# Float32 products with v for a pair of heads in turns, split scores from the second chunk on, and own buffers for the preparation of weights

## The chip, the cores and the metric

The kernel runs on one core of a Trainium2 chip. The metric is the device time of one execution in microseconds (us), a median over runs. The engines are named as in the profile: PE (TensorE, with PEld for its weight loads), DVE (VectorE), ACT (ScalarE), POOL (GpSimd) and SP (SyncE, whose queue issues every DMA here).

## The reference, cut to what matters

```python
# q, k, v: (4, 8, 576, 64) float32;  w_in (512, 2048) and w_out (2048, 512) of both MLPs: float64
scores = q @ k.T / sqrt(64)                        # per batch and head, 576 x 576
kth    = the 32nd largest score of each row
attn   = softmax over the scores >= kth            # the others count as nothing
x      = attn @ v, heads side by side              # 2304 rows of 512
h = x @ w_in1;  x = (h - tanh(h)) @ w_out1         # first MLP
h = x @ w_in2;  y = elu(h) @ w_out2                # second MLP
```

## The kernel before

The 2304 rows are cut into six chunks of 384 tokens. Chunk ci's two MLPs run beside the attention of chunk ci+1, so there are seven stages: attention alone, five stages of both, and the last MLPs alone.

Products are made in one of two ways. As a *split* product, each float32 operand is the sum of two parts of type float32r, and TensorE makes one pass for each pair of parts. As a *plain float32* product, the operands stand as they are, and the profile shows each as two matmuls (passes) of its own. The MLPs are split everywhere: `first` makes 12 passes of 384 columns for an f-tile (128 of the 2048 hidden rows), `second` 9 passes of 512 columns. One f-tile is a step, and there are 32 steps to a chunk.

Attention goes in units of three query tiles of 128 rows: one head of a pair where a chunk lies in one batch (chunks 0, 2, 3 and 5), both heads of a pair with 192 queries each where it lies in two (chunks 1 and 4). There are eight units to a chunk, two to a pair of heads. A unit passes through:

- `load_q`, `load_k`, `split_qk`: operands of the scores. In a split unit q and k are loaded twice, onto both halves of the partitions, and ACT and POOL make the parts. `WHOLE = 2` makes chunks 0 and 1 plain float32, without parts.
- `scores`: one plain product (L253) or two split passes (L255, L256) for each half of the keys, and a copy by ACT.
- `topk_steps`: four rounds of MAX8 and MATCH_REPLACE8 on DVE, in four ticks. The last masks the weights: DVE alone (L289), or DVE, POOL and ACT in a row (L283 to L286) for the first `MASK_GP[ci]` tiles of a unit.
- `transposed`: five blocks of keys, turned by PE (L311) and copied by ACT. In a split unit ACT copies twice (L312, L315) and POOL subtracts (L317).
- `attend`: products with v, once for each unit. Plain: five blocks of two passes into 64 of the 128 PSUM partitions, one head after the other (L332). Split: `split_v` puts v's two parts side by side, and nine passes give both (L342), which ACT and DVE then add (L350, L351).
- `norm`, `finish_pair`: division by the sums of weights, once for a pair, and the two parts of x.

The weights arrive as float64. `prepare` turns a half of an f-tile into float32 in integer arithmetic and splits it: 64 times in all, in the first two stages. Its operations are ACT (L136, L137, L142), DVE (L139), POOL (L143) or DVE (L145), POOL (L146), then the split (L107, L108). Its four kinds of buffers are shared with attention's split operands (tags `kk`, `qs`, `praw`, `vv`).

A tick is a quarter of a unit's top-k search. The program issues work tick by tick, and the Tile framework's scheduler sets the order on each engine from that with its own estimate of costs; on the chip each engine then follows that order. All DMAs are on SP's queue, in order; a load that waits for its buffer holds back those behind it.

Of the kernel before, what the change touches and what calls it, by code (L numbers as in the profile page):

```python
# [11 lines left out]
U32 = mybir.dt.uint32  # L12
AF = mybir.ActivationFunctionType
# [9 lines left out]
TOPK = 32  # L23
# [5 lines left out]
N = 384  # L29
FILL = -1.0e38  # L30

# A chunk of N tokens is a list of pieces (batch, first query, number of queries).
# [17 lines left out]
LOW_GP = range(0, 24)  # L50
# [10 lines left out]
WP_BUFS = 1  # L61
KK_BUFS = 4
QS_BUFS = 2
PR_BUFS = 4
VV_BUFS = 4
S_BUFS = 6

# Blocks of keys transposed in a tick; the tick of the products with v, counted from a unit's start.
PT_PER = 3
AV_AT = 7  # L70
# Ticks from the end of a chunk's top-k searches to the start of its MLPs: of the first chunk, and of the others.
DONE0 = 4
DONE = 8
# [3 lines left out]
def tile_topk_attention_two_mlps(  # L77
# [42 lines left out]
    weights, loads = {}, [(ci, m, ft) for ci in range(len(CHUNKS)) for m in range(2) for ft in range(NF)]  # L120
# [4 lines left out]
    def prepare(m, ft, half, stay=True):  # L125
# [4 lines left out]
        raw = sb.tile([P, 576], mybir.dt.int64, tag="kk", name=f"wr{m}_{ft}_{half}", bufs=KK_BUFS)[:, :512]  # L130
        nc.sync.dma_start(raw, (w1, w2)[m][ft][:, half * 512 : half * 512 + 512])
        words = raw.bitcast(F32).rearrange("p (n w) -> p n w", w=2)
        scaled = sb.tile([P, 512], F32, tag="qs", name=f"wsc{m}_{ft}_{half}", bufs=QS_BUFS)
        sign = sb.tile([P, 768], BF16, tag="praw", name=f"wsg{m}_{ft}_{half}", bufs=PR_BUFS)[:, :512]
        w = sb.tile([P, 640], F32, tag="vv", name=f"wf{m}_{ft}_{half}", bufs=VV_BUFS)[:, :512]
        nc.scalar.activation(scaled, words[:, :, 1], copy, scale=2.0**-112)  # L136
        nc.scalar.activation(sign, words[:, :, 1], AF.Sign)  # L137
        bits, wu, low = scaled.bitcast(U32), w.bitcast(U32), words.bitcast(U32)[:, :, 0]
# [8 lines left out]
        if stay:  # L147
            wt = weight_tile(half, f"wp{m}_{ft}_{half}")
        else:
            wt = sb.tile([P, 2, 512], F32R, tag="wp", name=f"wp{m}_{ft}_{half}", bufs=WP_BUFS)  # L150
        split(wt[:, 0], wt[:, 1], w)
        nc.sync.dma_start(f(scratch[m, ft, half]), f(wt))
        return wt
# [11 lines left out]
    def hurried(u):  # L165
# [7 lines left out]
    units, x_tiles, xuns, pair_units, chunk_end = [], {}, {}, {}, []  # L173
    for ci, pieces in enumerate(CHUNKS):
        for p in range(NPAIR):
            c0 = 0
            for b, q0, nq in pieces:
                for heads in ([[0], [1]] if nq >= 256 else [[0, 1]]):
                    u = Unit()
                    u.ci, u.b, u.p, u.q0, u.heads, u.c0 = ci, b, p, q0, heads, c0  # L180
                    u.id = f"{ci}_{p}_{b}_{heads[0]}"
                    u.n = nq
                    u.whole = ci < WHOLE
                    u.last = False
                    u.rush = ci == 0 and p == NPAIR - 1
                    units.append(u)
                    pair_units.setdefault((ci, p), []).append(u)
                c0 += nq
            units[-1].last = True
        chunk_end.append(len(units))  # L190

    def load_q(u):
        u.qraw = sb.tile([P, N], F32, tag="qraw", name=f"qraw{u.id}", bufs=2)
        src = qT[u.b, 2 * u.p + u.heads[0] : 2 * u.p + u.heads[-1] + 1, :, u.q0 : u.q0 + u.n].rearrange("h d s -> d h s")
        for half in range(1 if u.whole else 2):
            nc.sync.dma_start(u.qraw[half * D : half * D + D].rearrange("d (h s) -> d h s", s=u.n), src)

    def load_k(u):
        u.kraw = {}
        for h in u.heads:  # L200
            u.kraw[h] = sb.tile([P, S], F32, tag="kraw", name=f"kraw{u.id}_{h}", bufs=2)
            for half in range(1 if u.whole else 2):
                nc.sync.dma_start(u.kraw[h][half * D : half * D + D], kT[u.b, 2 * u.p + h])

    def split_qk(u):
        """q's parts stand over each other, k's parts twice: two products give all four terms."""
# [3 lines left out]
        u.qs = sb.tile([P, 512], F32R, tag="qs", name=f"qs{u.id}", bufs=QS_BUFS)[:, :N]  # L210
        nc.scalar.activation(u.qs, u.qraw, copy)
        nc.gpsimd.tensor_sub(u.qs[D:P], u.qraw[D:P], f(u.qs[D:P]))
# [5 lines left out]
    def load_v(u):  # L218
        u.vraw = {}
        for h in u.heads:  # L220
            u.vraw[h] = sb.tile([P, NB, D], F32, tag="vraw", name=f"vraw{u.id}_{h}")
            nc.sync.dma_start(u.vraw[h], vL[u.b, :, 2 * u.p + h])

    def split_v(u):
        """The main part stands in the head's own columns of its pair, the rest in the other's."""
        if u.whole:
            return
        u.vv = {}
        for h in u.heads:
            u.vv[h] = sb.tile([P, NB, 2, D], F32R, tag="vv", name=f"vv{u.id}_{h}", bufs=VV_BUFS)  # L230
            split(u.vv[h][:, :, h, :], u.vv[h][:, :, 1 - h, :], u.vraw[h])
# [27 lines left out]
    def topk_steps(u, r):  # L259
        """Round r of the top-k search of a unit's three tiles; the last one masks the weights."""  # L260
        if r == 0:
            u.vm = sb.tile([P, 3, 2, 8], F32, tag="vm", name=f"vm{u.id}")
            u.mb = sb.tile([P, 3], F32, tag="mb", name=f"mb{u.id}")
            u.sum = sb.tile([P, 3], F32, tag="sum", name=f"sum{u.id}", bufs=6)
            u.w = [sb.tile([P, S], F32, tag="w3", name=f"w3{u.id}_{t}", bufs=3) for t in range(3)]
        if r == 1:
            u.e = [sb.tile([P, S], F32, tag="e", name=f"e{u.id}_{t}", bufs=6) for t in range(3)]

        by_pool = 0 if u.rush else MASK_GP[u.ci]

        def find(t):
            nc.vector.max(u.vm[:, t, min(r, 1)], u.s[t] if r == 0 else u.w[t])  # L272
            if r == 0 and t == 2:
                nc.gpsimd.tensor_scalar_mul(u.mb, u.vm[:, :, 0, 0], -SCALE)
            if r == 1 and t >= by_pool:
                nc.scalar.activation(u.e[t], u.s[t], AF.Exp, bias=u.mb[:, t : t + 1], scale=SCALE)  # L276

        def drop(t):
            v = u.vm[:, t, min(r, 1)]
            if r < 3:  # L280
                nc.vector.match_replace(u.w[t], v, u.s[t] if r == 0 else u.w[t], FILL)  # L281
            elif t < by_pool:
# [331 lines left out]
```

## Time and profile before

| | |
|---|---|
| median of 3 runs | 1304.95 us (1304.8 to 1308.14) |
| profiled execution: span | 1304.7 us, so 0.2 us lie around the span against the median |
| PE busy | 1222.4 us, 94% of the span |
| DVE busy | 1063.8 us, 82% |
| ACT busy | 868.7 us, 67% |
| POOL busy | 832.6 us, 64% |
| mean granted PE clock | 0.959 of full speed |

Busy shares are averages over seven stages, each with a limit of its own. A matmul's end is modelled, so the time between the starts of two matmuls tells more than the length shown for one.

### The profile page before, as it was taken

How to read it: one execution, taken by the hardware profiler on the slowest of the kernel's cores; microseconds unless marked ns; L12 is line 12 of the kernel's file. 1: busy time of each engine (PE TensorE's matmuls, PEld its weight loads, DVE VectorE, ACT ScalarE, POOL GpSimd, SP SyncE). 2: the span in 40 equal slices, each digit the busy share in tenths (PEclk: the TensorE clock that was granted, in tenths of full speed). 3: DMA queues.
4: the chain of work that ended last, by engine and by line, in shares of the span. 5: the costliest groups of instructions: out<-in, count | busy, mean ns of one | idle time of the engine just before them, and what ended most of it. 6: DMA issues, size and time to landing. Idle time of an engine off the chain costs nothing.

```text
span 1304.7 us, 20365 instructions
## 1 busy us (share of the span) xinstructions
PE 1222.4 (94%) x6384; PEld 1022.2 (78%) x6384; DVE 1063.8 (82%) x2118; ACT 868.7 (67%) x1932; POOL 832.6 (64%) x779
## 2 busy tenths in 40 slices
PE   5756899998998999999999999998999999999998
PEld 2323457775777899899998999997899989999897
DVE  7989989979999999999999899899999999110111
ACT  7767647878786766777767777668677666542333
POOL 6888309997888777667665667666666663533222
PEclk9866689998998999999999999999999999999999
DMA  6456217876587977576866677675666654577672
GB/s 217 166 180 211 83 35 236 287 250 225 173 280 250 315 238 230 171 235 211 269 213 204 219 237 257 226 238 169 220 228 232 215 193 167 203 264 259 212 253 77
DMA packets 93675, 278.83 MB, mean 214 GB/s; under 512 B 11392, under 2 KB 26240, under 8 KB 93568
## 3 DMA queue, kind: packets, MB, share of 16 engines
q1 hardware_dynamic: 93568, 277.52, 63.8%
q8 instruction: 52, 0.85, 0.3%
q14 instruction: 55, 0.45, 0.1%
HBM read 239.21 MB, written 38.27 MB: 213 GB/s over the span
## 4 chain that ended last, share of the span: by engine, by line
PE 79%; DVE 10%; ACT 6%; issue 2%; DMA 2%; POOL 1%; SPq 0%; POOLq 0%; ACTq 0%; DVEq 0%
PE h L409 30%; PE acc L443 28%; PE pt L311 5%; PE av L342 4%; PE av L332 4%; DVE vm L272 3%; PE ps L253 3%; DVE w L281 3%; DMA wr<-in_w_dram 2%; PE ps L255 2%; PE ps L256 2%; DVE wf L139 1%; DVE wf L145 1%; DVE e L289 1%; ACT y L457 1%
## 5 line engine op out<-in xcount | busy, mean ns | idle before, releaser
L272 DVE MAX8 vm<-w 128x8 f32<-128x576 f32 x432 | 320.7, 751 | 5.4
L108 POOL TENSOR_TENSOR gl<-g,gh 128x384 fp32r<-128x384 f32 x192 | 202.7, 1056 | 170.5 <-ACT gh L107 140.8
L443 PE MATMUL acc<-wt,gh 128*128 128x512 f32 x984 | 269.1, 397 | 1.1 <-ACT gh L107 1.1
L281 DVE MATCH_REPLACE8 w<-vm,w 128x576 f32<-128x576 f32 x288 | 213.1, 740 | 0.1
L443 PEld LDWEIGHTS acc<-wt,gh 128*128 128x128 f32 x984 | 177.9, 188 | 28.1 <-ACT gh L107 2.2
L257 ACT ACTIVATE s<-ps 128x288 f32<-128x288 f32 (+1 forms) x320 | 125.8, 407 | 63.8 <-PE ps L256 37.5
L317 POOL TENSOR_TENSOR pl<-pr,ph 128x384 fp32r<-128x384 f32 x128 | 134.6, 1065 | 47.8 <-ACT pr L315 46.3
L311 PE MATMUL pt<-ident,e 128*128 128x128 f32 (+1 forms) x720 | 120.3, 293 | 40.2 <-ACT e L285 32.0
L443 PE MATMUL acc<-wt,gl 128*128 128x512 f32 x492 | 148.4, 398 | 0.3 <-POOL gl L108 0.3
L409 PE MATMUL h<-xh,wt 128*128 128x384 f32 x672 | 145.6, 340 | 0.0
L107 ACT ACTIVATE gh<-g 128x384 fp32r<-128x384 f32 x192 | 101.6, 529 | 64.7 <-DVE g L422 31.6
L311 PEld LDWEIGHTS pt<-ident,e 128*128 128x128 f32 (+1 forms) x720 | 89.3, 142 | 70.6 <-ACT e L285 35.5
L312 ACT ACTIVATE ph<-pt 128x384 fp32r<-128x384 f32 (+3 forms) x240 | 115.8, 492 | 42.8 <-PE pt L311 42.0
L409 PE MATMUL h<-zh,wt 128*128 128x384 f32 (+2 forms) x720 | 141.6, 326 | 2.7 <-ACT zh L462 2.3
L272 DVE MAX8 vm<-s 128x8 f32<-128x576 f32 x144 | 107.9, 749 | 29.2 <-ACT s L257 28.9
L422 DVE SCALAR_TENSOR_TENSOR g<-t,h 128x384 f32<-128x384 f32 x96 | 52.3, 545 | 94.3 <-ACT t L415 90.9
L409 PEld LDWEIGHTS h<-xh,wt 128*128 128x128 f32 x672 | 118.8, 188 | 7.9 <-issue 0.8
L409 PEld LDWEIGHTS h<-zh,wt 128*128 128x128 f32 x720 | 118.0, 189 | 8.3 <-ACT zh L462 3.5
L289 DVE SCALAR_TENSOR_TENSOR e<-s,vm,e 128x576 f32<-128x576 f32 x118 | 115.0, 979 | 2.8 <-ACT e L276 2.4
L253 PE MATMUL ps<-kraw,qraw 64*128 64x288 f32 x224 | 97.7, 561 | 19.0 <-ACT ph L312 9.5
L281 DVE MATCH_REPLACE8 w<-vm,s 128x576 f32<-128x576 f32 x144 | 106.6, 741 | 0.0
L427 DVE TENSOR_TENSOR g<-h,t 128x384 f32<-128x384 f32 x84 | 46.0, 548 | 69.8 <-ACT t L412 68.8
(90 smaller groups left out, 2558.5 us busy)
## 6 DMA issues: line engine op xcount, KB each, us to landing
wt<-w SPq DMA_DIRECT2D x328, 512.0 KB, 4.2
wr<-in_w_dram SPq DMA_DIRECT2D x64, 512.0 KB, 5.0
w<-wp SPq DMA_DIRECT2D x64, 512.0 KB, 4.1
kraw<-in_kT_dram SPq DMA_DIRECT2D x104, 144.0 KB, 3.9
vraw<-in_vL_dram SPq DMA_DIRECT2D x64, 160.0 KB, 3.7
qraw<-in_qT_dram SPq DMA_DIRECT2D x80, 96.0 KB, 3.8
out_dram<-o SPq DMA_DIRECT2D x5, 768.0 KB, 5.0
out_dram<-o SPq DMA_DIRECT2D x3, 256.0 KB, 2.2
```

Source lines behind the costliest of these rows:

```text
L107: nc.scalar.activation(hi, src, copy)
L108: nc.gpsimd.tensor_sub(lo, src, f(hi))
L253: nc.tensor.matmul(pt[:, :HS], u.qraw[0:D, qc], u.kraw[h][0:D, cs], start=True, stop=True)
L257: nc.scalar.activation(s[lo:hi, cs], pt[lo:hi, :HS], copy)
L272: nc.vector.max(u.vm[:, t, min(r, 1)], u.s[t] if r == 0 else u.w[t])
L281: nc.vector.match_replace(u.w[t], v, u.s[t] if r == 0 else u.w[t], FILL)
L289: nc.vector.scalar_tensor_tensor(u.e[t], u.s[t], v[:, 7:8], u.e[t], op0=ALU.is_ge, op1=ALU.mult, accum_out=u.sum[:, t : t + 1])
L311: nc.tensor.transpose(pt[:kn, t * P : t * P + P], u.e[t][:, k0 : k0 + kn], ident)
L312: nc.scalar.activation(u.ph[:kn, blk], pt[:kn, :N], copy)
L317: nc.gpsimd.tensor_sub(low, raw[:kn], f(u.ph[:kn, blk]))
L409: nc.tensor.matmul(h[:, cs], wv[:, wi, kt], xs[:, kt, cs], start=(a == 0), stop=(a == len(jobs) - 1))
L443: nc.tensor.matmul(acc[ci, m][:, t], gx[:, t * P : t * P + P], wt[:, wi], start=(ft == 0 and k == 0), stop=(ft == NF - 1 and k == 2),)
```

## The change

1. `WHOLE` goes from 2 to 1: chunk 1's scores are split like those of chunks 2 to 5.
2. Products with v are plain float32 in all chunks. `split_v`, the second copy, POOL's subtraction and the sum of two parts are gone.
3. `attend` runs once for a pair, behind the pair's last unit, with the two heads' passes in turns, block by block; they go to the two halves of the PSUM partitions. One copy takes both. `ph` gets two buffers, v four.
4. `MASK_GP` is gone: DVE masks every tile (L289 of before).
5. `prepare` gets buffers of its own (three, two and two), writes the scaled words in place, lets ACT round all low words, and joins the words in one DVE instruction. Early tiles use the weights' own buffers.
6. `norm` adds 1e-9 on POOL and takes one reciprocal for a pair. `GATE_GP` is [0, 0, 1, 1, 1, 2]. The result of a chunk is stored tile by tile.
7. Loads of v are issued three ticks after a unit's start (before: one tick in split units, four in plain ones; in the first chunk's last unit one, as before), and loads of q and k eight ticks ahead in chunk 1 (before: six).

```diff
-WHOLE = 2
-MASK_GP = [3, 0, 0, 1, 0, 0]
-GATE_GP = [0, 1, 0, 0, 0, 2]
+GATE_GP = [0, 0, 1, 1, 1, 2]
...
+RAW_BUFS = 3
+KK_BUFS = 3
+VR_BUFS = 4
+PH_BUFS = 2
+WHOLE = 1
...
-        nc.vector.tensor_scalar(wu, bits, 3, None, op0=ALU.logical_shift_left)
-        if m * NF + ft in LOW_GP:
-            i32 = mybir.dt.int32
-            nc.scalar.activation(low.bitcast(i32), low, copy, scale=2.0**-29 * (1 - 2.0**-20), bias=-0.5 + 7.5 * 2.0**-20)
-            nc.gpsimd.tensor_tensor(w.bitcast(i32), w.bitcast(i32), low.bitcast(i32), op=ALU.add)
-        else:
-            nc.vector.scalar_tensor_tensor(wu, low, 29, wu, op0=ALU.logical_shift_right, op1=ALU.bitwise_or)
+        nc.scalar.activation(low.bitcast(I32), low, copy, scale=2.0**-29 * (1 - 2.0**-20), bias=-0.5 + 7.5 * 2.0**-20)
+        nc.vector.scalar_tensor_tensor(
+            w.bitcast(U32), scaled.bitcast(U32), 3, low, op0=ALU.logical_shift_left, op1=ALU.bitwise_or
+        )
         nc.gpsimd.tensor_mul(w, w, sign)
...
+        for c0, heads in pieces.items():
+            n = heads[0][0].n
+            pt = bank("at", f"av{ci}_{p}_{c0}", 3)
+            for blk, (_, kn) in enumerate(KBLK):
+                for h in range(2):
+                    v, cs = heads[h]
                     nc.tensor.matmul(
-                        pt[main, : u.n], u.vraw[h][:kn, blk], u.ph[:kn, blk, cs], start=(blk == 0), stop=(blk == NB - 1)
+                        pt[h * D : h * D + D, :n],
+                        v.vraw[h][:kn, blk],
+                        v.g.ph[:kn, blk, cs],
+                        start=(blk == 0),
+                        stop=(blk == NB - 1),
                     )
...
+            if hurried(u):
+                nc.vector.tensor_mul(xun[:, xs], pt[:, :n], u.rs[:, xs])
+            else:
+                nc.scalar.activation(xun[:, xs], pt[:, :n], copy)
...
+                nc.gpsimd.tensor_scalar_add(r[:, at : at + len(v.g.tiles)], v.g.sum[:, : len(v.g.tiles)], 1e-9)
...
+        nc.vector.reciprocal(r[:, :at], r[:, :at])
...
+            on(before, t0 + (1 if hurried(u) else 3), lambda u=u: load_v(u))
...
+            if u.last:
+                on(ends, t0 + 7, lambda u=u: norm(u.ci, u.p, u))
+                on(ends, t0 + 7, lambda u=u: attend(u))
+                on(ends, t0 + 7, lambda u=u: finish_pair(u))
```

## Rows read from the trace of the kernel before

**Rows 1.** Busy time by stage: window, length, engines (x instructions), PE clock, DMA.

```profile
0.00:186.80 186.80, 129.46 (x335) 64.55 (x336) 168.47 (x343) 121.30 (x263) 117.73 (x105) 0.76 0.45 153
...
186.80:445.40 258.60, 247.65 (x1244) 188.80 (x1244) 245.22 (x460) 201.09 (x425) 216.98 (x180) 0.97 0.73 244
445.40:1164.40 719.00, 711.91 (x4125) 649.84 (x4125) 634.90 (x1290) 498.94 (x1150) 459.96 (x458) 1.00 0.67 220
```

**Rows 2.** The chain that ended last: start us, us, what; products with v.

```profile
181.91 2.72 PE av L332 x8
...
185.31 0.79 PE av L332 x2
...
554.91 1.59 PE av L342 x9
...
828.56 2.19 PE av L342 x18
```

**Rows 3.** PE in order of time, chunk 1: 20 plain passes, two heads.

```profile
247.25 3.84 PE L332 MATMUL av<-ph,vraw 128*64 128x192 f32 x20
```

**Rows 4.** PE in order of time, chunk 4: L373's passes in 64-column halves.

```profile
827.62 0.94 PE L373 MATMUL rt<-ident,r 128*64 128x128 f32 x16
```

**Rows 5.** PE matmuls by form that overlap 827.60 to 827.70 us.

```profile
L373 PE MATMUL rt<-ident,r 128*64 128x128 f32 x1 | 0.3, 322 | 0.0
L373 PE MATMUL rt<-ident,r 128*64 128x64 f32 x1 | 0.3, 269 | 0.0
```

**Rows 6.** PE in order of time, chunk 2: two split passes of the scores, next matmul.

```profile
645.21 0.29 PE L255 MATMUL ps<-kk,qs 128*128 128x288 f32 x1
...
645.48 0.39 PE L443 MATMUL acc<-wt,gh 128*128 128x512 f32 x1
```

**Rows 7.** DVE groups, 186.8 to 445.4 us: busy us, mean ns, idle before.

```profile
L139 DVE TENSOR_SCALAR wf<-wsc 128x512 uint32<-128x512 uint32 x41 | 35.6, 869 | 0.8 <-ACT wsc L136 0.8
L289 DVE SCALAR_TENSOR_TENSOR e<-s,vm,e 128x576 f32<-128x576 f32 x28 | 31.2, 1121 | 1.7 <-ACT e L276 1.7
...
L145 DVE SCALAR_TENSOR_TENSOR wf<-wr,wf 128x512 uint32<-128x512 uint32 x16 | 17.8, 1111 | 0.0
...
L359 DVE TENSOR_SCALAR r<-sum 128x3 f32<-128x3 f32 x10 | 4.6, 459 | 0.5 <-PE rt L373 0.5
```

**Rows 8.** Durations of two DVE lines: min/median/max ns, over the whole span.

```profile
L289 DVE SCALAR_TENSOR_TENSOR e<-s,vm,e x118: 781/810/1841, 143.9 to 1109.6; 128x576 f32<-128x576 f32 x118
...
L145 DVE SCALAR_TENSOR_TENSOR wf<-wr,wf x16: 667/1106/1830, 337.7 to 414.9; 128x512 uint32<-128x512 uint32 x16
```

**Rows 9.** POOL groups, 186.8 to 445.4 us.

```profile
L108 POOL TENSOR_TENSOR wp<-wf,wp 128x512 fp32r<-128x512 f32 x45 | 63.2, 1405 | 18.5 <-ACT wp L107 18.4
L146 POOL TENSOR_TENSOR wf<-wf,wsg 128x512 f32<-128x512 f32 x41 | 51.9, 1270 | 4.8 <-DVE wf L145 4.0 <-ACT wsc L136 0.7
...
L143 POOL TENSOR_TENSOR wf<-wf,wr 128x512 int32<-128x512 int32 x25 | 34.7, 1390 | 2.8 <-DVE wf L139 2.8
L108 POOL TENSOR_TENSOR kk<-kraw,kk 128x576 fp32r<-128x576 f32 x6 | 8.8, 1460 | 0.0
```

**Rows 10.** ACT groups, 186.8 to 445.4 us.

```profile
L142 ACT ACTIVATE wr<-wr 128x512 int32<-128x512 uint32 x21 | 14.0, 667 | 0.0
...
L107 ACT ACTIVATE kk<-kraw 128x576 fp32r<-128x576 f32 x7 | 4.8, 688 | 1.1 <-DVE wf L145 1.0
```

**Rows 11.** DVE groups, 0 to 186.8 us.

```profile
L139 DVE TENSOR_SCALAR wf<-wsc 128x512 uint32<-128x512 uint32 x23 | 15.5, 673 | 0.5 <-ACT wsc L136 0.5
L283 DVE TENSOR_SCALAR w<-s,vm 128x576 f32<-128x576 f32 x18 | 13.5, 751 | 0.0
...
L359 DVE TENSOR_SCALAR r<-sum 128x3 f32<-128x3 f32 x8 | 3.5, 443 | 0.0
L281 DVE MATCH_VALUE_LOAD w<-vm,s 128x8 f32 x27 | 2.1, 79 | 5.0 <-ACT e L285 4.9
```

**Rows 12.** Waits of SP's queue: us in total, times, longest us.

```profile
SPq L222 <- PE av L332: 55.5, 22, 9.8
```

More of the change, by code (lines that the diff above doesn't have):

```diff
@@ L40 @@
 ]
-WHOLE = 2
-MASK_GP = [3, 0, 0, 1, 0, 0]
-GATE_GP = [0, 1, 0, 0, 0, 2]
-LOW_GP = range(0, 24)
+SIZES = [sum(n for _, _, n in c) for c in CHUNKS]
+NMAX = max(SIZES)
+GATE_GP = [0, 0, 1, 1, 1, 2]
 EARLY = range(12, 16)
@@ L119, in tile_topk_attention_two_mlps, with prepare @@
     }
-    weights, loads = {}, [(ci, m, ft) for ci in range(len(CHUNKS)) for m in range(2) for ft in range(NF)]
+    weights, loads = {}, [(ci, m, ft) for ci in range(len(SIZES)) for m in range(2) for ft in range(NF)]
     def weight_tile(half, name):
         return sb.tile([P, 2, 512], F32R, tag=f"w{half}", name=name, bufs=(WI_BUFS, WO_BUFS)[half])
-    def prepare(m, ft, half, stay=True):
-        raw = sb.tile([P, 576], mybir.dt.int64, tag="kk", name=f"wr{m}_{ft}_{half}", bufs=KK_BUFS)[:, :512]
+    def prepare(m, ft, half):
+        raw = sb.tile([P, 512], I64, tag="wr", name=f"wr{m}_{ft}_{half}", bufs=RAW_BUFS)
@@ L163, in load_next @@
                 nc.sync.dma_start(f(wt), f(scratch[m, ft, half]))
+    class Unit:
+        pass
+    class Group:
+        pass
+    units, groups, pair_units, pair_end, chunk_end = [], [], {}, {}, []
+    x_tiles, xuns = {}, {}
+    for ci, size in enumerate(SIZES):
+        for p in range(NPAIR):
+            row = []
+            c0 = 0
+            for b, q0, n in CHUNKS[ci]:
+                for heads in ([[0], [1]] if n >= 256 else [[0, 1]]):
+                    u = Unit()
+                    u.ci, u.b, u.p, u.q0, u.heads, u.c0, u.n = ci, b, p, q0, heads, c0, n
+                    u.id = f"{ci}_{p}_{b}_{q0}_{heads[0]}"
+                    u.whole = ci < WHOLE
+                    u.last = False
+                    u.k = n * len(heads) // P
+                    row.append(u)
+                c0 += n
+            pair_units[ci, p] = row
+            units += row
+            cuts, k = [], 0
+            for u in sorted(row, key=lambda u: -u.k):
+                for g in cuts:
+                    if sum(v.k for v in g) + u.k <= 3:
+                        g.append(u)
+                        break
+                else:
+                    cuts.append([u])
+            for us in cuts:
+                g = Group()
+                g.units, g.at, g.id = us, len(groups), f"{ci}_{p}_{us[0].id}"
+                g.tiles = [(u, t) for u in us for t in range(u.k)]
+                g.rush = ci == 0 and p == NPAIR - 1
+                for u in us:
+                    u.g, u.j0, u.rush = g, sum(v.k for v in us[: us.index(u)]), g.rush
+                groups.append(g)
+            for u in groups[-1].units[-1:]:
+                u.last = True
+                pair_end[ci, p] = u
+        chunk_end.append(len(groups))
@@ L165, in hurried @@
     def hurried(u):
         return u.rush and u.last
-    class Unit:
-        pass
[L173 to L190, printed above, removed]
@@ L220, in load_v @@
         for h in u.heads:
-            u.vraw[h] = sb.tile([P, NB, D], F32, tag="vraw", name=f"vraw{u.id}_{h}")
+            u.vraw[h] = sb.tile([P, NB, D], F32, tag="vraw", name=f"vraw{u.id}_{h}", bufs=VR_BUFS)
             nc.sync.dma_start(u.vraw[h], vL[u.b, :, 2 * u.p + h])
[L224 to L231, printed above, removed]
     def segments(u, t):
@@ L257, in scores, with topk_steps @@
                 nc.scalar.activation(s[lo:hi, cs], pt[lo:hi, :HS], copy)
-    def topk_steps(u, r):
+    def topk_steps(g, r):
+        k = len(g.tiles)
         if r == 0:
[L262 to L265, printed above, removed]
+            g.vm = sb.tile([P, 4, 2, 8], F32, tag="vm", name=f"vm{g.id}")
+            g.mb = sb.tile([P, 4], F32, tag="mb", name=f"mb{g.id}")
+            g.sum = sb.tile([P, 4], F32, tag="sum", name=f"sum{g.id}", bufs=8)
+            g.w = [sb.tile([P, S], F32, tag="w3", name=f"w3{g.id}_{j}", bufs=W_BUFS) for j in range(k)]
@@ L266, in topk_steps @@
         if r == 1:
[L267 to L276, printed above, removed]
@@ L370, in norm @@
                 continue
-            for t in range(3):
+            for t in range(v.k):
                 for lo, hi, h, c in segments(v, t):
@@ L433, in second @@
     def second(ci, m, ft):
+        nt = SIZES[ci] // P
         if ft == 0:
@@ L437, in second @@
         gh, gl = parts.pop((ci, m, ft))
-        jobs = [(k, t) for k in range(3) for t in range(3)]
+        jobs = [(k, t) for k in range(3) for t in range(nt)]
         if ft == NF - 1:
@@ L466, in store @@
         a = acc.pop((ci, 1))
-        y = sb.tile([P, 3, 512], F32, tag="y", name=f"o{ci}", bufs=1)
-        rows = out[ci * N : ci * N + N].rearrange("(t p) e -> p t e", p=P)
-        last = ci == len(CHUNKS) - 1
-        for t in range(3):
-            nc.scalar.activation(y[:, t], a[:, t], copy)
-            if last:
-                nc.sync.dma_start(rows[:, t], y[:, t])
-        if not last:
-            nc.sync.dma_start(rows, y)
+        nt = SIZES[ci] // P
+        y = [sb.tile([P, 512], F32, tag="y", name=f"o{ci}_{t}", bufs=Y_BUFS) for t in range(SIZES[ci] // P)]
+        spans, c0 = [], 0
+        for b, q0, n in CHUNKS[ci]:
+            while n:
+                k = min(n, P - c0 % P)
+                spans.append((c0 // P, c0 % P, k, b * S + q0))
+                c0, q0, n = c0 + k, q0 + k, n - k
+        for t in range(nt):
+            nc.scalar.activation(y[t], a[:, t], copy)
+            for at, r0, k, row in spans:
+                if at == t:
+                    nc.sync.dma_start(out[row : row + k], y[t][r0 : r0 + k])
     def step_parts(i):
@@ L557, in tile_topk_attention_two_mlps @@
             if j == 0:
-                for t in range(3):
-                    on(tick, -4, t, lambda u, t=t: scores(u, t))
+                for do in mid.get(tick, ()):
+                    do()
             b()
```

282 lines of the change are left out of this document (136 added, 146 removed).

## The prediction

> **What bounds the kernel now.** I began with busy time by stage, cut where the first chunk's x is ready (186.8 us) and where the results of chunks 0 and 4 leave (445.4 and 1164.4 us) [rows 1]. The reader is to see three different kernels in it. From 445.4 to 1164.4 us, the four stages that hold the MLPs of chunks 1 to 4 and the attention of chunks 2 to 5, PE is busy for 711.9 of 719.0 us and DVE for 634.9: PE alone sets the time, a microsecond more of PE work is a microsecond of time, and work taken from the other engines returns at most the 7.1 us in which PE stood. From 186.8 to 445.4 us (MLP of chunk 0, attention of chunk 1, most of the weights' preparation) PE has 247.7, DVE 245.2, POOL 217.0 and ACT 201.1 of 258.6 us. There PE and DVE bound together, so relief of one is worth only what the other allows. Before 186.8 us DVE leads with 168.5 and PE, half idle, is granted 0.76 of its clock. The last stage, MLPs alone, isn't touched. Second, I read the prices of the products with v in the chain and in PE's order of time [rows 2, 3], and whether passes on the two halves of the PSUM partitions overlap anywhere [rows 4, 5]. Third came DVE, POOL and ACT by line in the second and the first stage [rows 7 to 11].
>
> **The products with v: what a pass costs.** At the end of the first stage a plain head of 384 queries takes 2.72 us for its eight passes over full blocks and 0.79 us for the two over the last, half block: 3.5 us, 0.34 us for a full pass [rows 2]. A split head takes 1.59 us for nine passes [rows 2]. So one plain head costs 2.2 times a split one, and everything hangs on whether two heads in turns run at once. Nothing in the kernel before makes these products in turns. The nearest row is L373, which also sends plain passes alternately wide into the two halves: 16 passes, eight of 128 columns and eight of 64, in at most 0.94 us [rows 4]. One after another, at 0.34 us for 384 columns, they would take 8 x 0.113 + 8 x 0.057 = 1.36 us. And in the first 0.1 us there starts, beside the first pass of 128 columns, one of 64 [rows 5], though the program has two of 128 first: it can only be of a later product. So the halves overlap in this kernel. In chunk 1 the program lists one head's ten passes and then the other's; 20 passes of 192 columns take 3.84 us [rows 3], no better than 20 x 0.17 = 3.4 us in a row. Turns are what is new. I take full overlap plus 0.2 us for filling and draining: 3.7 us a pair of 384, about 2.0 us a piece of 192 (half of 3.84, and a little). Bounds: 3.5 us, and 7.0 us for no overlap.
>
> The Trainium skill (PSUM — Partial Sum Buffer, "Engine vs sequencer instructions") says that matmuls start and complete in program order. The pass of 64 columns that starts within the first 0.1 us speaks against it here; by that rule turns would still overlap, with one pass of lag in every group.
>
> **What that adds and takes, by stage.** Chunks 2, 3 and 5 have 12 pairs: before 2 x 1.59 = 3.2 us, after 3.7, so +6 us; without overlap +3.8 x 12 = +46. Chunk 4: 18 passes of two heads take 2.19 us before [rows 2], eight times 17.5 us; after 8 x 2.0 = 16, so -1.5; without overlap 8 x 3.84 = 30.7, so +13. Chunk 1: eight times 3.84 = 30.7 before, 16 after, so -15; without overlap 0. Chunk 0 isn't PE-bound; only its last pair counts, where before just the second head's 3.5 us stood at the end and now the pair's 3.7 does: nothing with overlap, +3.5 without.
>
> **Chunk 1's scores.** 64 plain products of two passes of 288 columns, 0.34 x 288/384 = 0.255 us each, are 33 us. Split, two passes take 0.27 us from the first start to the next matmul [rows 6], 64 x 0.27 = 17: PE -16 us. With -15 from above PE has some 217 of the second stage's work left, and DVE alone bounds it.
>
> **The second stage on DVE.** The preparation there now takes 41 L139 (35.6 us) and 16 L145 (17.8) [rows 7]; after, one instruction of L145's kind each. L145 lasts from 0.667 us to 1.83, mean 1.11 [rows 7, 8]; which it is goes with POOL's business, as for L289, whose median is 0.81 over all and whose mean here is 1.12. POOL stays as busy: it loses 25 L143 (34.7 us) and gains chunk 1's parts of k and q, 16 x 1.46 and 8 of two thirds of that, 31 us [rows 9]. I take 1.05 us: 43 us for 53.4, -10 (bounds -26 and -8). L359 leaves, -4.6 [rows 7]. DVE goes from 245 to 230 us; at today's share of 95% the stage would take 243 us, -15. But ACT, 201 us now, gains 20 roundings of 0.667 us and the copies of k (16 x 0.688) and q (8 of some 0.46) [rows 10]: 28 us, so 229 of 243, 94% where it had 78%. Every matmul's result goes through ACT, so some of the gain is lost in its queue: I take -12. Bounds: 0, and -28 if DVE's 13 us of idling goes too.
>
> **The first stage on DVE.** 23 L139 (15.5 us) become 23 instructions of 0.8 us (between L145's 0.667 and 1.11, POOL having lost its additions): +3. 18 L283 (13.5 us) become L289 at its median with the sum read out, 0.9 us: +2.7. Gone are L359 (3.5) and the 4.9 us in which DVE waited for the masked weights' exponentials [rows 11]. Together -3; bounds -8 and +5.
>
> **At nothing.** In the four PE-bound stages POOL's subtractions, ACT's second copies and DVE's sums leave engines that PE covers; I credit 2 of the 7.1 us in which PE stood. Loads of v move two ticks later, and in chunk 4 the next pair's may reach SP's queue ahead of the products that free its buffer. Such waits exist, 55.5 us in 22, 9.8 at most [rows 12]; behind them stand weight loads, five f-tiles ahead, some 27 us, so nothing shows; without that cover each would cost its length, at most 9.8. Doubled q and k loads of chunk 1 use DMA that is busy 0.73 of the time [rows 1]. Fewer buffers for the preparation cost nothing while a half f-tile, every 258.6/41 = 6.3 us, holds a buffer over POOL's 1.27 and 1.41 us [rows 9] and the steps between; two buffers cover some 12 us.
>
> **Sum.** 1304.7 - 3 - 12 + 6 - 1.5 - 2 = 1292.2 us, and 0.2 around the span: 1292.
>
> **Rivals.** *No overlap.* The second head's passes wait for the first's, by a shared path that L373's short passes don't fill. Stages three to six get +59, the first +0.5, the second gains 10 on the scores and DVE: about 1352 us. Rows 4 and 5 speak against it; it decides as soon as a pair takes more than 4.7 us, where the 12 pairs alone eat the gain. *ACT holds the second stage.* Its 28 us more leave that stage where it is: 1304.7 - 3 + 4.5 - 2 = 1304 us. For it speaks that four engines are near full; against it, that ACT has 57 us free there now. *Passes start in program order.* A lag of 0.34 us on 12 pairs and 0.17 on chunk 4's eight pieces adds 5 us: 1298. This is what the Trainium skill's rule above would make of it.
>
> **Chances.** Forecast 0.60 (own range 1282 to 1301, the bounds of the first two stages drawn in); no overlap 0.10; ACT 0.20 (1299 to 1312); program order 0.05; more than the forecast, DVE's idling gone too, 0.05 (1276 to 1282). A range of 1276 to 1312 leaves out the first rival and the tails, somewhat under 2 in 10. Faster or slower by over 0.3%, about what a measurement of this kernel can tell from no change, is below 1301 or above 1309. Faster: 0.55 of the forecast, 0.04 of program order, 0.05, and 0.02 of ACT's, 0.66. Slower: 0.10, 0.07 of ACT's, and 0.03 for an order of work that the scheduler makes worse, 0.20. The same: 0.14.
>
> **What would show it.** Right: in chunks 2 to 5 the 20 passes of a pair span 3.5 to 4 us; chunk 1's scores show two short passes; the result of chunk 0 leaves near 430 us; the four stages behind take 719 to 724 us. Wrong: a pair near 7 us; a second stage of 255 us or more with ACT, or POOL behind it, ending PE's and DVE's waits; SP's waits for v in front of stalled weight loads; a first stage longer than 190 us, with DVE waiting for a buffer of the preparation.

## The result, and the profile after

The kernel after takes 1316.49 us (median of four runs, 1312.89 to 1318.28) against 1306.09 us for the kernel before beside it: a ratio of 1.0075, 95% interval 1.0056 to 1.0093. It is slower; 1292 us was forecast, and the range ended at 1312. The profiled execution's span is 1314.6 us.

Busy time by stage, of the kernel after, as in [rows 1]: the low part of the first chunk's x is written at 187.1 us (before at 189.2, 2.4 us behind the cut in [rows 1]), the results of chunks 0 and 4 leave at 436.8 and 1174.4 us.

```profile
0.00:187.10 187.10, 115.20 (x345) 60.49 (x346) 175.44 (x354) 120.28 (x245) 74.37 (x78) 0.78 0.49 158
187.10:436.80 249.70, 219.45 (x1257) 186.21 (x1256) 240.52 (x448) 217.13 (x456) 204.98 (x175) 0.93 0.77 258
436.80:1174.40 737.60, 727.15 (x4148) 620.80 (x4147) 587.13 (x1181) 420.94 (x929) 271.85 (x294) 1.00 0.67 215
1174.40:1314.60 140.20, 132.82 (x680) 117.99 (x678) 15.20 (x27) 46.85 (x95) 37.54 (x37) 0.99 0.63 208
```

Between these events the first stage went from 189.2 to 187.1 us, -2.1, and the second from 256.2 to 249.7, -6.5; the four PE-bound stages went from 719.0 to 737.6, +18.6, and the last one stayed. So 8.6 us were won up to chunk 0's result, and over twice that was lost behind it, where DVE (634.9 to 587.1 us), ACT and POOL all had less to do and PE more (711.9 to 727.2).

Those stages hold the 12 pairs of chunks 2, 3 and 5 and the four of chunk 4. PE in order of time, the kernel after, two of the 12 pairs (start us, us, line, operation; L337 are the products with v, L417 and L453 the MLPs' passes, L409 and L443 before):

```profile
445.84 2.15 PE L337 MATMUL av<-ph,vraw 128*64 128x384 f32 x10
447.92 1.66 PE L453 MATMUL acc<-wt,gh 128*128 128x512 f32 x6
449.42 0.86 PE L453 MATMUL acc<-wt,gl 128*128 128x512 f32 x3
450.21 0.87 PE L337 MATMUL av<-ph,vraw 128*64 128x384 f32 x4
451.01 1.66 PE L453 MATMUL acc<-wt,gh 128*128 128x512 f32 x6
452.51 0.86 PE L453 MATMUL acc<-wt,gl 128*128 128x512 f32 x3
453.30 1.65 PE L337 MATMUL av<-ph,vraw 128*64 128x384 f32 x6
454.88 0.62 PE L417 MATMUL h<-xh,wt 128*128 128x384 f32 x2
...
495.58 3.59 PE L337 MATMUL av<-ph,vraw 128*64 128x384 f32 x20
499.11 0.97 PE L417 MATMUL h<-xh,wt 128*128 128x384 f32 x4
```

The second pair runs as forecast: 3.52 us from its first start to the next matmul, for 20 passes. The first is cut in three by 18 passes of the second MLP. The same view between 495.57 and 495.70 us, by form, is the counterpart of [rows 5]: two passes of the pair start there at once.

```profile
L337 PE MATMUL av<-ph,vraw 128*64 128x384 f32 x2 | 0.5, 537 | 0.0
```

Their starts lie 7 ns apart, and the next two follow after 0.37 us. So a pair is ten rounds of two passes. They are one pass of each head: in the first experiment below, where the heads don't take turns, no two passes start so close.

For every pair I took the time from its first start to the matmul behind it, less 0.231 us for each pass of 512 columns (0.174 for one of 384) that stands in between:

| products with v, chunks 2 to 5 | before | after | forecast of the difference |
|---|---|---|---|
| 24 heads, or 12 pairs, of chunks 2, 3, 5 | 38.4 us (1.57 to 1.70 a head) | 51.6 us: four uncut pairs at 3.52, eight cut ones at 4.50 to 4.89 | +6 |
| chunk 4 | 16.2 us | 15.4 us (3.85 for 40 passes) | -1.5 |
| sum | 54.6 us | 67.0 us | +4.5 |

Whole pairs would make 42.2 us of the 51.6, so the cuts cost 9.4 us, 1.0 to 1.4 for each cut pair. The shortest cut shows where it goes; PE in order of time, the kernel after:

```profile
679.75 0.86 PE L337 MATMUL av<-ph,vraw 128*64 128x384 f32 x2
680.54 0.96 PE L453 MATMUL acc<-wt,gl 128*128 128x512 f32 x3
681.43 3.59 PE L337 MATMUL av<-ph,vraw 128*64 128x384 f32 x18
684.95 0.79 PE L417 MATMUL h<-xh,wt 128*128 128x384 f32 x3
```

The two passes in front are both passes of one head's first product: they start one after the other, 0.37 us apart, while the other head's product stands behind the cut. The trace of line L337, 679.5 to 680.4 us (ns at the least, median, most; first and last start):

```profile
L337 PE MATMUL av<-ph,vraw x2: 486/512/537, 679.8 to 680.1; 128*64 128x384 f32 x2
```

Among the 18 passes behind the cut two more start alone, 0.32 us apart, near the end, so those 18 take ten rounds and not nine. The pair has twelve rounds for ten. In each of the eight cut pairs just four passes start alone, whether it is cut once or twice: two rounds more, some 0.65 us. The rest is the change between passes on half the columns and on all 128: three passes of the MLP, 0.69 us at their usual pace, take 0.89 here, and the first round after the change is longer. A pair cut once takes 0.98 to 1.00 us more than a whole one, a pair cut twice 1.34 to 1.37. So of the 9.4 us some 5 are passes left without a partner and some 4 the twelve cuts themselves.

### The profile page after: what moved, and what is told of

Read it like the earlier page. It is cut to its first block, busy times and chain, and to the rows that moved or that the text cites. A ratio compares the mean times of both kernels' runs of the same rounds, so it can differ in the third digit from the quotient of the medians.

```text
span 1314.6 us, 19819 instructions
## 1 busy us (share of the span) xinstructions
PE 1194.6 (91%) x6424; PEld 985.5 (75%) x6424; DVE 1018.3 (77%) x2008; ACT 805.2 (61%) x1722; POOL 588.7 (45%) x584
## 4 chain that ended last, share of the span: by engine, by line
PE 66%; DVE 14%; ACT 8%; DMA 6%; issue 3%; POOL 3%; SPq 0%; POOLq 0%; ACTq 0%; DVEq 0%
PE h L417 27%; PE acc L453 25%; DVE vm L286 5%; PE av L337 5%; DVE w L296 5%; DMA wr<-in_w_dram 4%; PE pt L319 4%; PE ps L268 2%; PE ps L269 2%; DVE e L298 2%; DVE wf L143 1%; ACT wr L142 1%; ACT s L270 1%; POOL wp L112 1%; ACT wr L141 1%
## 5 line engine op out<-in xcount | busy, mean ns | idle before, releaser
L453 PE MATMUL acc<-wt,gh 128*128 128x512 f32 x984 | 266.7, 398 | 1.8 <-ACT gh L111 1.8
L453 PEld LDWEIGHTS acc<-wt,gh 128*128 128x128 f32 x984 | 180.0, 188 | 35.3 <-ACT gh L111 2.5
L319 PE MATMUL pt<-ident,e 128*128 128x128 f32 (+1 forms) x720 | 123.5, 296 | 74.9 <-DVE e L298 53.3
L111 ACT ACTIVATE gh<-g 128x384 fp32r<-128x384 f32 x192 | 100.5, 525 | 82.6 <-DVE g L431 42.2
L453 PE MATMUL acc<-wt,gl 128*128 128x512 f32 x492 | 150.3, 400 | 0.3 <-POOL gl L112 0.3
L320 ACT ACTIVATE ph<-pt 128x384 f32<-128x384 f32 (+1 forms) x240 | 109.3, 488 | 64.9 <-PE pt L319 63.8
L417 PE MATMUL h<-zh,wt 128*128 128x384 f32 (+2 forms) x720 | 142.6, 328 | 3.5 <-ACT zh L472 3.0
L417 PE MATMUL h<-xh,wt 128*128 128x384 f32 x672 | 141.1, 339 | 0.7 <-DVE g L431 0.7
L298 DVE SCALAR_TENSOR_TENSOR e<-s,vm,e 128x576 f32<-128x576 f32 x144 | 136.8, 957 | 3.0 <-ACT e L290 0.9
L417 PEld LDWEIGHTS h<-zh,wt 128*128 128x128 f32 x720 | 118.6, 190 | 14.3 <-ACT zh L472 3.9
L417 PEld LDWEIGHTS h<-xh,wt 128*128 128x128 f32 x672 | 117.4, 188 | 9.8 <-issue 2.4
L290 ACT ACTIVATE e<-s,mb 128x576 f32<-128x576 f32 x144 | 101.6, 770 | 28.7 <-POOL mb L288 28.4
L337 PE MATMUL av<-ph,vraw 128*64 128x384 f32 (+3 forms) x640 | 107.5, 440 | 0.0
L453 PEld LDWEIGHTS acc<-wt,gl 128*128 128x128 f32 x492 | 90.1, 188 | 20.8 <-POOL gl L112 1.9
```

Source lines behind the costliest of these rows:

```text
L111: nc.scalar.activation(hi, src, copy)
L290: nc.scalar.activation(u.e[t], u.s[t], AF.Exp, bias=g.mb[:, j : j + 1], scale=SCALE)
L298: nc.vector.scalar_tensor_tensor(u.e[t], u.s[t], v[:, 7:8], u.e[t], op0=ALU.is_ge, op1=ALU.mult, accum_out=g.sum[:, j : j + 1])
L319: nc.tensor.transpose(pt[:kn, j * P : j * P + P], v.e[t][:, k0 : k0 + kn], ident)
L320: nc.scalar.activation(g.ph[:kn, blk, :nq], pt[:kn, :nq], copy)
L337: nc.tensor.matmul(pt[h * D : h * D + D, :n], v.vraw[h][:kn, blk], v.g.ph[:kn, blk, cs], start=(blk == 0), stop=(blk == NB - 1),)
```

## The experiments

Two theories stood at the start. By *cut*, the halves overlap and PE's loss comes from foreign passes within a pair. By *turns*, the halves hinder each other and the price of the pair itself is wrong. For the second stage DVE, ACT, POOL and the buffers of the preparation were candidates.

**One head after the other.** The kernel after, with the two loops over blocks and heads exchanged:

```diff
-            for blk, (_, kn) in enumerate(KBLK):
-                for h in range(2):
+            for h in range(2):
+                for blk, (_, kn) in enumerate(KBLK):
```

> The changed kernel with one head's ten passes listed before the other's. If turns are what lets two heads run at once, a pair of 384 queries takes 7.0 us for 3.5, chunk 4's eight pieces 31 us for 15.5: the four PE-bound stages get some 45 to 57 us longer, the kernel takes 1360 to 1375 us. If passes on the two halves overlapped in any order, nothing changes (1316).

Measured: 1377.86 us, ratio 1.0552 (1.0534 to 1.0570). PE in order of time, an uncut pair of this kernel:

```profile
609.12 7.09 PE L337 MATMUL av<-ph,vraw 128*64 128x384 f32 x20
616.14 1.14 PE L417 MATMUL h<-zh,wt 128*128 128x384 f32 x5
```

7.02 us in a row, 3.52 in turns: the overlap is complete, and it is worth 61 us of the kernel. Nine pairs of 384 are cut here too, and cost only 0.24 to 0.42 us more than uncut ones, against 1.0 to 1.4 in turns: with no partners to lose, this is the price of the change alone. One that is cut as the pair at 679.75 us was takes 7.36 us without the three MLP passes, for 7.02:

```profile
504.77 0.86 PE L337 MATMUL av<-ph,vraw 128*64 128x384 f32 x2
505.56 0.96 PE L453 MATMUL acc<-wt,gl 128*128 128x512 f32 x3
506.45 6.45 PE L337 MATMUL av<-ph,vraw 128*64 128x384 f32 x18
512.83 0.80 PE L417 MATMUL h<-xh,wt 128*128 128x384 f32 x3
```

**Products ahead of the MLP's last part.** In the program a tick issues the third part of its MLP step, `c()`, just ahead of the pair's products. Here the products go first:

```diff
-            c()
             if j == 0:
                 for do in ends.get(tick, ()):
                     do()
+            c()
```

> The changed kernel with a pair's products issued ahead of the second MLP product of the same tick, where the changed one issues them behind it; the scheduler then leaves the passes together. Theory of the cut groups: the passes with v are parted by MLP passes, each cut drains the array and leaves a head's passes alone; then the products of chunks 2, 3 and 5 fall from 18.5 to some 14.5 us a chunk and the kernel takes 1304 to 1308 us. Theory of the price: plain passes cost that by themselves, and nothing changes (1316).

Measured: 1308.5 us, ratio 1.0008 (0.9999 to 1.0018): 8 us of the loss are gone. PE in order of time, the pair that was cut at 679.75 us in the kernel after, and the windows of this kernel's second stage and of the four PE-bound ones:

```profile
676.50 3.59 PE L337 MATMUL av<-ph,vraw 128*64 128x384 f32 x20
680.02 0.96 PE L453 MATMUL acc<-wt,gl 128*128 128x512 f32 x3
```

```profile
185.20:439.70 254.50, 220.00 (x1280) 184.91 (x1278) 244.31 (x458) 221.54 (x466) 207.38 (x180) 0.95 0.77 257
439.70:1165.70 726.00, 715.89 (x4125) 622.78 (x4125) 585.66 (x1171) 414.91 (x918) 267.79 (x290) 0.99 0.68 217
```

Eleven of the 12 pairs are whole now, at 3.52 us. The last is cut by 42 MLP passes into 8 and 12; there no pass starts alone, and it takes 3.91 us. The products with v of the 16 pairs take 58.0 us for 67.0, and the four stages 726.0 for 737.6. So the theory of the cut stands. The second stage is 4.8 us longer, and holds the first of the 12 pairs now, 3.5 us that left the four. Of the 7.0 us by which the four still exceed the kernel before, 3 are time in which PE stands (10.1 us for 7.1); PE's longest waits come at the turn from the first MLP to the second. The rest isn't told apart. PE's waits from the end of chunk 0 to that of chunk 4 (us in total, times, longest), of the kernel before, of the kernel after, and of this one:

```profile
PE yt L460 <- ACT y L457: 1.8, 3, 0.7
```

```profile
PE yt L470 <- ACT y L467: 3.9, 4, 2.4
PE h L417 <- ACT zh L472: 2.7, 3, 1.2
PE ps L268 <- DVE zl L473: 2.5, 2, 2.0
```

```profile
PE yt L470 <- ACT y L467: 5.9, 4, 2.7
PE h L417 <- ACT zh L472: 2.4, 2, 1.2
```

**Split products where one head fills a unit.** The kernel after, with the kernel before's transposes, split of v and split products in chunks 2, 3 and 5, and the pairs in turns in chunks 0, 1 and 4:

```diff
+PARTS = (2, 3, 5)
...
-                on(ends, t0 + 7, lambda u=u: attend(u))
+                on(ends, t0 + 7, lambda u=u: (attend_parts if u.ci in PARTS else attend)(u))
```

> The changed kernel with the split products with v of the kernel before in chunks 2, 3 and 5 alone; chunks 0, 1 and 4 keep the plain ones in turns. If the loss lies in those products (cut or price), the four PE-bound stages go back to some 720 us and the kernel takes 1298 to 1303 us, faster than before. If it lies elsewhere (attention's pace, loads, order of the MLPs), it stays at 1312 to 1318.

Measured: 1295.04 us, ratio 0.9921 (0.9905 to 0.9937). It beats both kernels. Windows, second stage and the four behind it:

```profile
183.80:437.50 253.70, 220.47 (x1261) 186.50 (x1260) 242.63 (x452) 220.78 (x466) 211.45 (x187) 0.94 0.78 259
437.50:1151.90 714.40, 707.15 (x4120) 640.73 (x4119) 608.87 (x1203) 475.34 (x1077) 406.19 (x427) 1.00 0.69 220
```

714.4 us for 719.0 before and 737.6 after, with 134 us more work on POOL than after: POOL has the room. The split heads are cut here as well, by up to 24 passes, and take 1.55 to 1.67 us apart from these, cut or not. A cut costs them nothing that can be read: they use all 128 columns, as the MLPs do, and have no partner to lose.

**Split products, ahead of `c()`.** The two edits above together; and, on top, a fourth buffer for the raw weights:

> The third experiment's kernel (split products with v in chunks 2, 3 and 5, plain ones in turns elsewhere) with the products issued ahead of the second MLP product, as in the second experiment. If cuts cost split products little, since they need no turns, and only chunks 1 and 4 gain: 1292 to 1297 us, as the third. If the order itself saves time everywhere: 1286 to 1291.

> The seventh's kernel with four buffers for the raw words, room for which comes from letting the small part of the products share a tag. If late raw words hold the second stage, 3 to 8 us below the seventh; else the same.

Measured: 1304.62 us (0.9981 to 0.9999) and 1311.61 us (1.0030 to 1.0054). With hardly a cut left that costs anything, the new order only does harm: the second stage takes 260.1 us for 253.7. The fourth buffer came with another edit (the products' second part shares a buffer with the transposes), so the 7 us that the two cost aren't told apart.

**Chunk 1's scores.** The kernel after with `WHOLE = 2`, plain scores in chunk 1 as before:

> The changed kernel with chunk 1's scores plain again (WHOLE = 2): PE gets 16 us more in the second stage, ACT some 15 and POOL some 31 us less. If DVE alone bounds that stage, as the prediction had it, nothing is lost: 1312 to 1317, the less POOL in DVE's way the better. If the split scores carried the second stage's gain, it gives it back: 1322 to 1330.

Measured: 1320.9 us, ratio 1.0112 (1.0098 to 1.0126), 4.4 us above the kernel after, between the two ranges expected. The second stage takes 253.2 us for 249.7 and the third 185.2 for 180.4; split scores in chunk 1 are a gain, a small one for 16 us of PE's work.

**Buffers of the preparation.** `RAW_BUFS` 3 to 5, the buffers of `wsg` and `wf` 2 to 4:

> The changed kernel with more buffers for the preparation of weights: five for the raw words (three) and four each for the signs and the words (two). If the second stage is held by raw words that land late because their buffer is freed late, it gets 4 to 10 us shorter: 1306 to 1312 us. If DVE's own work holds it, nothing changes: 1314 to 1318.

Measured: 1328.99 us, ratio 1.0173 (1.0158 to 1.0188). Both expectations missed: more buffers are worse. First stage 193.6 us (187.1), second 250.5 (249.7), third 184.6 (180.4). In the first stage, which DVE leads, two more joins run (23 for 21) and joins and masks take longer, 22.0 and 29.1 us for 18.3 and 27.4: 5.4 of its 6.5 us. Why they do wasn't tested.

**DVE's join, taken apart again.** One instruction of DVE's becomes a shift on DVE and an addition on POOL, for all 64 halves:

```diff
-        nc.vector.scalar_tensor_tensor(
-            w.bitcast(U32), scaled.bitcast(U32), 3, low, op0=ALU.logical_shift_left, op1=ALU.bitwise_or
-        )
+        nc.vector.tensor_scalar(w.bitcast(U32), scaled.bitcast(U32), 3, None, op0=ALU.logical_shift_left)
+        nc.gpsimd.tensor_tensor(w.bitcast(I32), w.bitcast(I32), low.bitcast(I32), op=ALU.add)
```

> The changed kernel with the words joined by a shift on DVE and an addition on POOL, as the kernel before did for 48 of the 64 halves, here for all 64. The prediction's term for the preparation: the join on DVE costs or saves little against a shift that waits for POOL, but POOL gets some 65 to 80 us more in the first two stages, three quarters of it in the second, where it has 49 us free: 1318 to 1328 us. If POOL has room enough, 1312 to 1317.

Measured: 1345.21 us, ratio 1.0301 (1.0288 to 1.0315). Window of the second stage:

```profile
179.40:487.80 308.40, 248.68 (x1382) 203.03 (x1381) 299.88 (x591) 244.76 (x520) 275.60 (x239) 0.93 0.65 219
```

DVE is busy for 97% of a stage that is 59 us longer, POOL for 89%. Little of DVE's work was for chunks 0 and 1: chunk 1's attention ended at 358 us (399 after, 423 before), and DVE searched for chunk 2, with 167 MAX8 in the stage for 122, until chunk 0's MLP was done. A busy share near full is no sign that the stage waits for DVE.

**Chunk 1's MLP three ticks sooner.** `DONE = [4, 5, 8, 8, 8, 8]` for `[4, 8, 8, 8, 8, 8]`, first in the kernel after, then with the split products:

> The changed kernel with the second chunk's MLPs due three ticks earlier (DONE 5 for 8), so that chunk 0's MLP steps are packed into 33 ticks for 36 and less of chunk 2's top-k search comes among them. Theory of running ahead: the 15 us that DVE gained in the second stage went in part into top-k search of chunk 2, which is worth nothing since PE alone holds the later stages; then the result of chunk 0 leaves 5 to 12 us earlier and the kernel takes 1304 to 1312 us. If the preparation holds chunk 0's MLP steps, 1313 to 1318.

> The third experiment's kernel (split products with v in chunks 2, 3 and 5) with the same three ticks: by running ahead 1283 to 1290 us, by the preparation 1293 to 1297.

Measured: 1318.58 us (1.0082 to 1.0109) and 1299.02 us (0.9926 to 0.9955): nothing gained. The second stage took 252.2 us and holds 87 + 30 MAX8 for 91 + 31 after (on replaced tiles, and on scores). So the new `DONE` kept only five of them out, and says little on whether it costs that DVE runs ahead with chunk 2.

**Heads in a row in chunks 0 and 1 alone**, with the split products elsewhere:

> The third experiment's kernel with the heads one after the other in chunks 0 and 1, so that turns are left in chunk 4 alone: PE gets 13 to 15 us more in the second stage and 3.5 at the end of the first. If DVE holds the second stage, as the prediction had it, 1296 to 1300 us; if PE's relief made its gain, 1306 to 1312.

Measured: 1313.53 us, ratio 1.0061 (1.0047 to 1.0075), 18 us above the split products with turns. The second stage takes 265.7 us for 253.7, the first 189.7 for 183.8, and PE is busy in the second for 236.9 us instead of 220.5. PE's relief was worth most of its length there, though PE stands for 30 of 250 us in the kernel after.

**Taking work from one engine at a time.** Three kernels that leave something out, each from the kernel after: ACT's rounding, POOL's product with the sign, and one of the three MATCH_REPLACE8 of a tile on DVE.

```diff
-        nc.scalar.activation(low.bitcast(I32), low, copy, scale=2.0**-29 * (1 - 2.0**-20), bias=-0.5 + 7.5 * 2.0**-20)
         nc.vector.scalar_tensor_tensor(
-            w.bitcast(U32), scaled.bitcast(U32), 3, low, op0=ALU.logical_shift_left, op1=ALU.bitwise_or
+            w.bitcast(U32), scaled.bitcast(U32), 3, scaled.bitcast(U32), op0=ALU.logical_shift_left, op1=ALU.bitwise_and
         )
```

(DVE's join stays, and reads the scaled words in place of the rounded ones.)

> The changed kernel without ACT's rounding of the low words (the weights miss their last three bits): ACT gets some 41 x 0.57 = 23 us less in the second stage. If ACT's queue holds that stage (187.1 to 436.8 us now), it gets 10 to 20 us shorter; if DVE or POOL does, under 5.

```diff
-        nc.gpsimd.tensor_mul(w, w, sign)
```

> The changed kernel without POOL's product with the signs (the weights lose their signs): POOL gets some 43 x 1.29 = 55 us less in the second stage, and stands less in DVE's way. If POOL holds the stage, it gets 15 us or more shorter; if ACT does, under 5; if DVE does, some 5 to 10, by the shorter joins.

```diff
+            if r == 2:
+                return
```

> The changed kernel without the third of the top-k search's three replacements (24 largest are kept for 32): DVE gets some 24 to 30 x 0.66 = 16 to 20 us less in each of the first five stages of attention. If DVE holds the second stage, as the prediction had it, that gets 14 to 20 us shorter and the first some 10 to 15; if ACT or POOL does, under 5. The later stages don't change, since PE alone holds them.

Measured: 1309.6 us (1.0010 to 1.0034), 1308.36 us (1.0003 to 1.0030) and 1295.67 us (0.9889 to 0.9963). Windows of the second stage, one fence for each, with the third stage behind in the first and the first stage ahead in the last; the kernel after has 987 PE instructions in its third stage, which takes 180.4 us:

```profile
186.00:435.50 249.50, 224.76 (x1304) 188.99 (x1303) 249.35 (x478) 203.28 (x434) 214.74 (x181) 0.95 0.75 254
435.50:609.60 174.10, 171.65 (x940) 146.30 (x939) 141.49 (x287) 95.12 (x211) 59.04 (x66) 1.00 0.68 233
```

```profile
183.20:423.00 239.80, 210.58 (x1214) 177.09 (x1213) 225.37 (x426) 208.81 (x441) 145.64 (x129) 0.94 0.78 266
```

```profile
0.00:170.50 170.50, 114.10 (x345) 62.12 (x346) 155.86 (x300) 118.65 (x245) 74.34 (x78) 0.77 0.53 174
170.50:422.40 251.90, 223.46 (x1280) 186.84 (x1279) 231.64 (x405) 221.25 (x467) 206.34 (x181) 0.94 0.75 257
```

With less on ACT the stage stays (249.5 us), but 47 of PE's instructions for chunk 2 moved into it, and the third stage, where PE bounds, is 6.3 us shorter. With less on POOL the second loses 10 us, of which the third gives 6 back (186.7 for 180.4), with 43 instructions moved the other way. With less on DVE the first stage loses 16.6 us, the second gains 2, and the third loses 2. So the second stage can't be judged by its length alone. Second and third together take 430.1 us after, 423.6 with less on ACT, 426.5 with less on POOL, 430.4 with less on DVE. DVE bounds the first stage, as argued, and its searches don't bound the second; ACT isn't ruled out there. Behind the third stage the last kernel still gains some: all four PE-bound stages take 730.2 us for 737.6, where nothing was expected.

**Moving POOL's work to DVE.** Two kernels from the split products: the low parts of chunk 1's k on DVE, and the low part of every second prepared half on DVE.

> The third experiment's kernel with the low parts of chunk 1's k made by DVE: POOL gets some 16 x 1.46 = 23 us less, most of it in the second stage, DVE some 16 x 0.7 = 11 us more. If POOL's queue holds that stage and DVE's fullness is work that runs ahead: 1286 to 1292 us; if DVE holds it: 1299 to 1308.

> The third experiment's kernel with the low part of every second prepared half made by DVE (those not prepared early): POOL gets some 28 x 1.4 = 39 us less in the first two stages, DVE some 28 x 0.65 = 18 us more. By POOL's queue 1285 to 1292 us, by DVE 1300 to 1312.

Measured: 1305.24 us (0.9979 to 1.0003) and 1323.62 us (1.0122 to 1.0155). The second stage takes 268.3 and 279.1 us for 253.7, second and third together 438.6 and 446.0 for 429.1. Had POOL alone held it, both had to gain.

## Why the prediction was wrong

**A pair's 20 passes stay together: the step that failed first.** "I take full overlap plus 0.2 us ... 3.7 us a pair" was right for the overlap (3.52 us, and 7.02 without) and for chunk 4 (3.85 for a pair's 40 passes, 4.0 forecast; the kernel before takes 2.0 us there for 18 passes, not the 2.19 of the one row read, so 0.8 us were won and not 1.5). It took for granted that a pair's passes would stand side by side in PE's order. They are issued in the same tick as an MLP step, and the scheduler put 3 to 42 foreign passes into eight of the 12 pairs. It does so before as well, which I could have seen, but there a cut is free. PE in order of time, the kernel before: a split head's nine passes with nine of the MLP among them, its first and the matmul behind it.

```profile
575.78 0.34 PE L342 MATMUL av<-ph,vv 128*128 128x384 f32 x1
...
579.43 0.33 PE L409 MATMUL h<-zl,wt 128*128 128x384 f32 x1
```

These are 3.65 us, and 1.57 without the nine at 0.231 us each, as for a whole head. In turns a cut costs 1.0 to 1.4 us: products with v +12.4 us for +4.5. The exchange of products and `c()` takes 9.0 of that away, and 11.6 us of the four stages, of which 3.5 are the pair that moved ahead of them.

The Trainium skill (TensorEngine Tiling (Array Packing), "Key Properties") says that different tiles of the array can load and multiply in parallel, and that a change of the tiling mode drains TensorE. The first agrees with this trace, 3.52 us for 7.02. The second agrees as far as a cut costs passes on half the columns time and passes on all of them none. It gives the drain no length; the nearest figure here is the 0.24 to 0.42 us of a cut pair with its heads in a row, where no pass loses a partner.

**Stalls of the PE-bound stages.** I credited 2 us of the 7.1 in which PE stood. The rest of the +18.6, 6 us, went the other way: PE stands for 10.5 us, +3.4, above all at the turn of the MLPs (for ACT's y 1.8 to 3.9 us, for DVE's zl 2.5 where it was none); some +1.5 us came ahead of the first pass of each group of products, which now changes to half the columns, and some +1.8 us in the distances between MLP passes in a row. That work taken from DVE, ACT and POOL returns little there was right: the 66 us that DVE has less without the third replacement returned 7. What widens the distances and the waits stays open.

**The second stage: the step that failed second.** -15 with DVE as the only bound, -12 taken; measured -6.5. DVE's and PE's sizes were right. DVE's groups of the stage, the kernel after, beside [rows 7]:

```profile
L286 DVE MAX8 vm<-w 128x8 f32<-128x576 f32 x91 | 66.4, 746 | 0.4
...
L143 DVE SCALAR_TENSOR_TENSOR wf<-wr 128x512 uint32<-128x512 uint32 x43 | 44.9, 1045 | 6.3 <-POOL wp L112 4.5 <-POOL wf L146 1.8
L298 DVE SCALAR_TENSOR_TENSOR e<-s,vm,e 128x576 f32<-128x576 f32 x29 | 32.1, 1114 | 0.0
```

The join takes 1.045 us (1.05 forecast), 44.9 us for 43, and PE is busy for 219 us (217 forecast). ACT has 217 us for the 229 forecast, POOL 205 for 217. What failed is "DVE alone bounds it". Part of DVE's relief went into search for chunk 2 (91 + 31 MAX8, before 87 + 30), chunk 1's attention ended 23 us sooner, at 399, and chunk 0's MLP still left at 437. PE's work in the second and third stages fell by 21.6 us (419.0 to 397.4), and PE stands 20.5 us longer in them (12.2 to 32.7). Over half of its 30 us in the second stage go to one wait: its transposes of the softmax weights wait for ACT's copies of scores, which free their PSUM banks. PE's longest wait of the second stage, after, and the same wait before:

```profile
PE pt L319 <- ACT s L270: 16.1, 8, 3.6
```

```profile
PE pt L311 <- ACT s L257: 1.9, 2, 1.4
```

So much of PE's relief turned into waiting for ACT's queue, which I had as a rival and as 3 us. Whether ACT is itself the bound, or is late by what it waits for, isn't settled. Without ACT's roundings this wait is 8.7 us, and the second and third stages together are 6.5 us shorter; the stage itself stays. Less POOL work shortens it by 10 us, more lengthens it by 59; but work moved from POOL to DVE lengthens it by 15 and 25, and 16 us more on PE by 12. The chain by which a half is prepared crosses ACT, DVE, POOL, ACT and POOL again, in queues that are each over 80% full, so a step late on any of them is late on all. That this is the bound was only argued.

**First stage.** -2.1 for -3: the right way, and bound by DVE, as the kernel with one replacement less showed. But those of the kernels above that are alike up to there (the kernel after, products first, split products, chunk 1's MLP sooner) take 183.8 to 187.1 us, so the size says little.

**At nothing.** Waits of SP's queue, the kernel after, the counterpart of [rows 12]:

```profile
SPq L135 <- DVE wf L143: 80.9, 38, 6.0
...
SPq L244 <- PE av L337: 58.9, 24, 18.3
```

The wait for v's buffers is twice as long at its worst, 18.3 us for 9.8, and PE's waits in the PE-bound stages name no DMA: the weights loaded ahead did cover it. Whether fewer buffers for the preparation were a loss wasn't tested by itself; more of them were one.

**The sum.** 1292.2 + 0.9 (first stage) + 5.5 (second) + 16.1 (the four behind) = 1314.7, against a span of 1314.6. Rivals: no overlap fell; passes in program order, by the rule on matmuls of the Trainium skill (PSUM — Partial Sum Buffer, "Engine vs sequencer instructions"), would have made a pair 3.9 us, and a pair of ten rounds and 3.52 us, whose first two passes start 7 ns apart, one of each head, speaks against it. The order that the scheduler makes worse had 0.03; it was the case, and it stood in no term of the sum.

## What to carry to other kernels

When two heads in turns depend on their passes standing side by side, price also what the scheduler may put between them, and issue them where nothing else is ready to go in; the trace of before shows whether it cuts such groups. Where a cut can't be avoided, let it fall between whole rounds and not between two partners (0.4 us for 1.0). Plain float32 in turns pays where it replaces a plain product or 18 short split passes (chunks 0, 1 and 4), and not where a split product already uses all columns (3.52 us for 3.2 a pair, before cuts): that mix was the best kernel, at 0.992 of before. Where four engines are over 80% busy, try each by taking a little work from it before you credit a microsecond, and read the gain over the stage and the next, since work moves across the cut; DVE's busy share of 96% did not make it the bound here.

## What was not expected of the hardware

- Plain float32 passes of two heads on opposite column halves overlap in full: 20 passes of 384 columns in 3.52 us in turns, 7.02 in a row, starts 7 ns apart.
- A cut between partners costs twice: four passes then start alone, two rounds more (some 0.65 us), and each change between half-column and full-column passes costs some 0.35. A pair cut once takes 1.0 us more, and 0.39 where the cut leaves the partners together; the same cut costs passes on all columns nothing.
- More buffers made the kernel slower: five and four for three and two, +12.5 us against the kernel after. Whether that comes from the chip or from the order that the scheduler then makes isn't known. A fourth for the raw weights came out 7 us slower too, together with a buffer shared elsewhere.
